# One chunked-attention and feed-forward kernel, its hand-written order of 801 steps replaced: v of the second unit behind the first weight cast on ScalarE, and all sequences, banks and engines drawn anew from there

## The chip, the cores and the metric

The kernel runs on one core of one Trainium2 chip. The metric is device time in microseconds, the median of several runs. A core has TensorE (PE, the matrix engine), VectorE (DVE), ScalarE (ACT), GpSimd (POOL) and SyncE (SP), which here only issues transfers; ACT issues transfers too. Each engine works through its own instructions in order, and waits on semaphores for the others.

## The reference

Inputs are q, k, v and alpha of 4 batches, 8 heads, 768 positions and 48 numbers a head, and four weight matrices. First a gated recurrence with a state of 48 x 48 for each head, then a feed-forward part whose hidden layer is the largest of three products:

```
for t in range(S):
    state = alpha[:, :, t, :, None] * state + einsum('bhd,bhe->bhde', k[:, :, t], v[:, :, t])
    y[:, :, t] = einsum('bhd,bhde->bhe', q[:, :, t], state)
x = y.transpose(0, 2, 1, 3).reshape(B * S, H * D)          # 3072 x 384
h = maximum(maximum(x @ w1, x @ w2), x @ w3)                # 3072 x 768
out = h @ w_out                                             # 3072 x 384
```

## The kernel before

The 768 positions are cut into 6 chunks of 128, and a **unit** is one chunk of one batch with its 8 heads: 24 units, numbered chunk by chunk, so units 0 to 3 are the first chunk of the four batches. Two units make a group, for which alpha, q, k and v are loaded: "load v 0 8" is v of the second half of group 0, which is v of unit 1. The first four groups are loaded in halves of 192 KB, the others in one piece of 384 KB.

For a unit u the steps are: "ln" (ACT, L402) takes logarithms of alpha; "cums u" (PE, L442) sums them along the chunk; "ep u" and "en u" (ACT, L447 and L450) are exponentials of these sums; "q~ u" and "k~ u" (L454, POOL or DVE) multiply q and k with them; "turn u" (PE, L483) transposes both and "qkT u" (L490, DVE or ACT) copies them out; "scores u" (PE, L499) multiplies them; "LA u" (DVE, L504) masks the scores; "v u" (L461 on ACT, L464 on POOL) scales v; "outs u" (PE, L542 and L545) makes the unit's output; "xb u" scales it (ACT L556, DVE L558); "x turn u" (PE, L572) and "xT u" (L577) transpose it for the second part. "totals", "e", "G", "sums", "U" and "Z" carry the state from chunk to chunk. In some late units a DMA transpose on SP ("cross u", "cross x u") stands in for PE's.

The second part takes the largest of three products as a sum: with differences wd = w2 - w1 and w3 - w1, the result is x w1 + max(0, x wd1, x wd2), so "grow u q g" (PE, L642) makes a product with one difference g of piece q, "relu" (ACT, L653) takes the first from 0 up and "max" (DVE, L658) takes the second in. The x w1 part is folded into one matrix w1 x w_out ("w1 turn", L366; "w1T", L372; "fold", L383; "w1o", L390). "shrink u" (PE, L678) makes the output rows, "ob u" (L693) copies them from PSUM and "store u" (L698) sends them off. Units 0 to 3, 22 and 23 go through this part alone, the rest in pairs.

The weights come in two column pieces, 0 to 256 (384 KB) and 256 to 768 (768 KB): "weights g p" is piece p of matrix g, where 0, 1, 2 are w1, w2, w3 and 3 is w_out. They arrive as fp32. "cast 0 p" and "cast 3 p" (ACT, L333) turn w1 and w_out into fp16, and "sub g p" (DVE or POOL, L341) makes the difference from the fp32 piece and the cast of w1. "grow" of a piece waits for its sub, the folds for all of the casts of w_out and the three w1T.

At the start PE also runs 27 "zeros" (L586): products of zeros, whose result nothing reads.

The order is written out by hand. The program enumerates 801 steps; ORDER is the list in which they are issued, and so fixes the sequence on each engine; PICK says for which steps the second of the offered engines is taken; BANKS gives each PSUM tile one of 8 banks (scores take two), in the order in which the tiles are enumerated. A tile that takes a bank waits until the readers of its former tile are done. The transfers of SP and ACT begin in the order of the list.

```
for i in ORDER:
    how, _, run, deps, _, _ = self.steps[i]
    e = how[PICK.get(i, 0)][0]
    ins = run(e)
```

Both kernels have the same steps, and so the same arithmetic and transfers.

Of the kernel before, what the change touches and what calls it, by code (L numbers as in the profile page):

```python
# [15 lines left out]

CDEC = 0.92
SIG = 128.0

NBANKS = 8  # L20
LEAD = (2.0, 4.0, 6.5, 5.0)
# [11 lines left out]


ORDER = (
# [44 lines left out]
)  # L80
BANKS = (
# [9 lines left out]
)  # L91
PICK = {
# [8 lines left out]
}  # L101


TRANSFERS = ("load", "weights", "cross", "store")
BEHIND = mybir.DependencyInfo(mybir.DependencyClass.NoSync, mybir.DependencyReason.DATA)
HARD, HARD_LOAD, HARD_LATE, LATE_FROM = 0.5, 1.8, 1.5, 3


# [18 lines left out]
class Plan:  # L127
# [31 lines left out]
    def issue(self, place):  # L159
        place.update(zip(self.users, BANKS))  # L160
        done, began = set(), []
        for i in ORDER:
# [4 lines left out]
            ins = run(e)  # L167
            if e != "POOL" and self.names[i].split()[0] in TRANSFERS:
                began.append(ins.ins)
# [5 lines left out]
def kernel(  # L175
# [41 lines left out]
    c32_np = np.stack(  # L217
        [SIG / dec, dec / SIG, np.full(P, HALF * np.log(CDEC))], axis=1
    ).astype(np.float32)
# [520 lines left out]
    for one, other in zip(began, began[1:]):  # L740
        tc.add_manual_dep(other, one.name, BEHIND, reason="transfers begin in the order of the plan")
# [28 lines left out]
```

## Time and profile before

| | before |
|---|---|
| median of 3 runs | 153.72 us (151.42 to 154.11) |
| profiled execution, device time | 150.59 us |
| its span in the profile | 148.8 us |
| PE busy | 133.9 us, 90% |
| DVE busy | 106.9 us, 72% |
| ACT busy | 90.5 us, 61% |
| POOL busy | 52.5 us, 35% |
| DMA | 31.07 MB, mean 209 GB/s |

A row of the timeline has the start, the duration, the engine (with a q where its queue issues a transfer), the line, the operation, what it writes and reads, the shape, the count, and in brackets how long the engine had been idle and what ended that. A row of the transfers ends with the us from issue to landing. A row of a stretch has, after its bounds and length, the busy us (and instructions) of PE, PE's weight loads, DVE, ACT and POOL, then the granted PE clock, the DMA engines' busy share and GB/s. A row of the groups has the instructions that share line, engine and shape, with their sum and the mean ns of one. Rows of the chain of waits have the start, the us, the engine and the line. The span runs from the first instruction to the last; the device time has some more around it.

### The profile page before, as it was taken

How to read it: one execution, taken by the hardware profiler on the slowest of the kernel's cores; microseconds unless marked ns; L12 is line 12 of the kernel's file. 1: busy time of each engine (PE TensorE's matmuls, PEld its weight loads, DVE VectorE, ACT ScalarE, POOL GpSimd, SP SyncE). 2: the span in 40 equal slices, each digit the busy share in tenths (PEclk: the TensorE clock that was granted, in tenths of full speed). 3: DMA queues.
4: the chain of work that ended last, by engine and by line, in shares of the span. 5: the costliest groups of instructions: out<-in, count | busy, mean ns of one | idle time of the engine just before them, and what ended most of it. 6: DMA issues, size and time to landing. Idle time of an engine off the chain costs nothing.

```text
span 148.8 us, 4162 instructions
## 1 busy us (share of the span) xinstructions
PE 133.9 (90%) x1683; PEld 104.6 (70%) x1683; DVE 106.9 (72%) x186; ACT 90.5 (61%) x184; POOL 52.5 (35%) x75
## 2 busy tenths in 40 slices
PE   0575297999999999999999999999999999999991
PEld 0233266968787886888787797787878877689781
DVE  7239318487998898979697779998578878584140
ACT  3531976948667587797746686745475844554331
POOL 0050041202523414840597709448029290170000
PEclk9999659999999999999999999999999999999999
DMA  5999999999999999999999999899998999704322
GB/s 115 205 225 322 202 341 269 283 267 173 223 208 219 237 220 210 248 184 250 266 266 263 185 197 250 163 215 269 177 232 160 243 325 189 147 4 131 109 82 79
DMA packets 116131, 31.07 MB, mean 209 GB/s; under 512 B 109712, under 2 KB 114960, under 8 KB 116112
## 3 DMA queue, kind: packets, MB, share of 16 engines
q1 hardware_dynamic: 83888, 21.17, 69.7%
q10 hardware_dynamic: 32224, 9.64, 28.7%
q8 instruction: 13, 0.21, 0.6%
q14 instruction: 6, 0.05, 0.1%
HBM read 23.69 MB, written 4.72 MB: 191 GB/s over the span
## 4 chain that ended last, share of the span: by engine, by line
PE 85%; SPq 5%; DMA 4%; ACT 2%; DVE 2%; issue 0%; ACTq 0%
PE psum L642 33%; PE psum L678 24%; PE psum L499 5%; PE psum L483 4%; SPq L308 4%; DMA vn<-in_v_dram 4%; PE psum L545 3%; PE psum L572 3%; PE psum L442 3%; PE psum L542 2%; PE psum L604 2%; PE psum L383 2%; PE psum L586 2%; PE psum L412 1%; DVE wd L341 1%; ACT w1h L333 1%
## 5 line engine op out<-in xcount | busy, mean ns | idle before, releaser
L642 PE MATMUL psum<-xT,wd 128*128 128x256 f16 (+1 forms) x540 | 54.4, 251 | 0.9 <-DVE wd L341 0.9
L642 PEld LDWEIGHTS <-wd 128*128 128x128 f16 x540 | 42.9, 98 | 6.9 <-DVE wd L341 1.7
L658 DVE TENSOR_TENSOR hT<-psum,hT 128x512 f16<-128x512 f32 (+1 forms) x39 | 24.3, 644 | 10.3 <-PE psum L642 4.7
L504 DVE TENSOR_TENSOR LA<-psum,c 128x1024 f16<-128x1024 f32 x24 | 28.6, 1219 | 3.1 <-PE psum L499 2.5
L653 ACT ACTIVATE hT<-psum 128x512 f16<-128x512 f32 (+1 forms) x39 | 21.5, 570 | 14.6 <-PE psum L642 13.6
L678 PE MATMUL psum<-wo,hT 128*128 128x384 f16 (+1 forms) x150 | 27.7, 320 | 0.0
L617 POOL TENSOR_TENSOR Z<-U,G 48x192 f16<-48x192 f32 x29 | 16.4, 572 | 12.5 <-DVE U L611 11.4
L678 PEld LDWEIGHTS <-hT 128*128 128x128 f16 x150 | 14.5, 98 | 8.9
L454 POOL TENSOR_TENSOR qk<-qn,ep 128x384 f16<-128x384 f32 x11 | 10.9, 998 | 15.1 <-ACT ep L447 13.3
L678 PE MATMUL psum<-w1o,xT 128*128 128x384 f16 (+1 forms) x75 | 15.8, 319 | 0.0
L450 ACT ACTIVATE en<-psum 128x384 f32<-128x384 f32 x24 | 11.9, 495 | 4.3 <-PE psum L442 3.8
L402 ACT ACTIVATE la<-an 128x384 f16<-128x384 f32 (+1 forms) x16 | 10.8, 689 | 5.7 <-DMA an<-in_alpha_dram 5.7
L454 POOL TENSOR_TENSOR qk<-kn,en 128x384 f16<-128x384 f32 x8 | 8.3, 1042 | 16.6 <-ACT en L450 12.7
L556 ACT ACTIVATE xb<-psum,c 128x384 f16<-128x384 f32 x16 | 9.1, 582 | 8.0 <-PE psum L545 5.8
L447 ACT ACTIVATE ep<-psum 128x384 f32<-128x384 f32 x24 | 11.7, 496 | 2.6 <-DVE qk L454 0.9
L693 ACT COPY ob<-psum 128x384 f32<-128x384 f32 (+1 forms) x18 | 8.3, 468 | 7.8 <-PE psum L678 5.1
L442 PE MATMUL psum<-la,c 128*128 128x384 f16 x24 | 7.8, 347 | 5.6 <-ACT la L402 5.5
L461 ACT ACTIVATE v<-vn,c 128x384 f16<-128x384 f32 x14 | 8.3, 614 | 6.2 <-DMA vn<-in_v_dram 6.2
L545 PE MATMUL psum<-v,LA 128*128 128x48 f16 x192 | 11.1, 186 | 0.0
L611 DVE TENSOR_TENSOR U<-psum,Z 128x384 f32<-128x384 f32 x16 | 8.5, 551 | 3.1 <-PE psum L604 2.5
L545 PEld LDWEIGHTS <-LA 128*128 128x128 f16 x192 | 9.8, 98 | 0.6 <-issue 0.2
L464 POOL TENSOR_SCALAR v<-vn,c 128x384 f16<-128x384 f32 x10 | 6.3, 635 | 9.4 <-DMA vn<-in_v_dram 9.0
(61 smaller groups left out, 189.6 us busy)
## 6 DMA issues: line engine op xcount, KB each, us to landing
out_dram<-ob ACTq DMA_DIRECT2D x20, 192.0 KB, 3.3
an<-in_alpha_dram SPq DMA_DIRECT2D x7, 384.0 KB, 6.6
ws<-in_moe_w_dram SPq DMA_DIRECT2D x3, 768.0 KB, 6.1
kn<-in_k_dram SPq DMA_DIRECT2D x5, 384.0 KB, 6.5
vn<-in_v_dram ACTq DMA_DIRECT2D x5, 384.0 KB, 6.6
an<-in_alpha_dram SPq DMA_DIRECT2D x8, 192.0 KB, 4.0
kn<-in_k_dram SPq DMA_DIRECT2D x8, 192.0 KB, 4.4
qn<-in_q_dram ACTq DMA_DIRECT2D x4, 384.0 KB, 5.3
```

The source lines that it names most:

```text
L402: lambda e, lo=lo * H, hi=hi * H: nc.scalar.activation(out=la[:, lo:hi, :D], in_=an[:, lo:hi, :], func=AFT.Ln, scale=1.0 / CDEC),
L442: nc.tensor.matmul(live[Lk], tri, la[:, hs, :D], start=True, stop=True)
L447: lambda e: nc.scalar.activation(out=ep, in_=live[Lk], func=AFT.Exp),
L450: lambda e: nc.scalar.activation(out=en, in_=live[Lk], func=AFT.Exp, scale=-1.0),
L454: lambda e, w=w, x=x, d=d: engines[e].tensor_mul(qk[:, w, :, :D], ld[x][n % LOADED][:, hs], d),
L504: lambda e: nc.vector.tensor_mul(LA.rearrange("p a b t -> p (a b) t"), live[Ak].rearrange("p a (b t) -> p (a b) t", t=P), maskA.unsqueeze( ...
L545: nc.tensor.matmul(yp[:, 2 * j + p, :], LA[:, p, j, :], v16[:, 2 * j + p, :], start=(cb == 0), stop=True, skip_group_check=True)
L617: lambda e, rows=rows, cols=cols: engines[e].tensor_mul(Zn[rows, :, cols], (Us[u % 3] if cb else live[pk])[rows, :, cols], G[rows, i * NP: ...
L642: nc.tensor.matmul(live[gk][:, jj, :], wd[:, kt, g, j * P:(j + 1) * P], xT[:, kt, :], start=(kt == 0), stop=(kt == NFT - 1))
L653: lambda e, h=h, gk=gk: nc.scalar.activation(out=h, in_=live[gk], func=AFT.Relu),
L658: lambda e, h=h, gk=gk: nc.vector.tensor_max(h, live[gk], h),
L678: nc.tensor.matmul(live[ok][:, cols], a[:, i * P:(i + 1) * P], w[:, cols], start=(kt == 0), stop=(kt == nk - 1))
```

## The change

ORDER, BANKS and PICK are replaced; two definitions move up in the file. The steps that are issued stay the same 801. 77 of them go to another engine, and 214 of 251 PSUM tiles to another bank. The heads of the lists:

```
 ORDER = (
-    4, 8, 9, 5, 6, 0, 10, 12, 34, 7, 32, 1, 11, 2, 123, 65, 127, 82, 84, 128, 129, 83, 64, 131,
-    86, 130, 85, 92, 115, 117, 98, 103, 104, 97, 95, 93, 68, 99, 133, 88, 110, 36, 37, 3, 42,
-    13, 87, 124, 70, 69, 35, 132, 33, 44, 73, 134, 89, 96, 106, 135, 90, 112, 56, 100, 136, 91,
...
+    5, 0, 8, 4, 12, 9, 2, 34, 6, 10, 11, 1, 37, 3, 32, 7, 65, 124, 64, 123, 82, 127, 83, 84,
+    129, 128, 86, 85, 131, 130, 92, 105, 104, 108, 99, 103, 97, 68, 88, 66, 116, 112, 94, 133,
+    106, 89, 132, 70, 69, 35, 72, 134, 71, 135, 90, 13, 36, 14, 136, 91, 42, 74, 93, 54, 107,
...
 BANKS = (
-    7, 1, 7, 7, 1, 4, 1, 3, 4, 3, 3, 4, 1, 2, 4, 6, 5, 0, 4, 3, 7, 0, 1, 5, 2, 5, 4, 6, 1, 5, 5,
...
+    3, 6, 3, 0, 1, 6, 0, 4, 2, 5, 4, 4, 0, 2, 3, 1, 2, 5, 2, 7, 7, 6, 7, 7, 7, 5, 4, 5, 5, 1, 4,
...
 PICK = {
-    27: 1, 30: 1, 44: 1, 71: 1, 72: 1, 75: 1, 85: 1, 86: 1, 87: 1, 132: 1, 138: 1, 140: 1, 144:
...
+    27: 1, 30: 1, 45: 1, 71: 1, 72: 1, 73: 1, 79: 1, 85: 1, 87: 1, 130: 1, 140: 1, 170: 1, 173:
...
```

Read as names, by following the enumeration, the fronts of the sequences are these (aN, kN, qN, vN: a load of unit N; Wgp: weights g p):

| | before | after |
|---|---|---|
| SP | a1 a2 k2 k1 q1 a0 q2 a3 W01 v1 W00 k0 v2 q0 W10 W11 v0 W31 k3 q3 W30 W21 W20 a4 | k1 a0 a2 a1 a3 k2 q0 W01 q1 q2 v2 k0 W11 v0 W00 v1 k3 W10 q3 W31 W30 W21 W20 a4 |
| ACT | ln 2, ln 1, en 1, ep 2, en 2, ep 1, ln 0, v 1, ln 3, en 0, ep 0, cast 0 1, v 2, cast 0 0, ep 3, qkT 0, xb 1, w1T 2, xT 2, w1T 1, w1T 0, e 1, xb 0, en 3, relu 2 1, cast 3 1, relu 1 1, e 0, relu 2 0, relu 1 0, cast 3 0 | ln 1, ln 3, ln 0, ln 2, ep 1, en 1, en 2, ep 2, en 0, ep 0, cast 0 1, w1T 1, xb 2, e 0, v 1, v 0, xb 1, en 3, cast 0 0, ep 3, w1T 2, relu 1 1, xT 2, e 1, w1T 0, cast 3 1, cast 3 0, relu 1 0, relu 2 1, relu 2 0, relu 0 0 |
| DVE | k~ 1, q~ 1, qkT 2, qkT 1, LA 2, LA 1, k~ 0, q~ 0, xb 2, LA 0, xT 1, sub 1 1, xT 0, q~ 3, qkT 3, LA 3, sub 2 1, sub 2 0 | q~ 1, q~ 2, qkT 1, k~ 0, qkT 2, q~ 0, LA 2, LA 1, qkT 0, LA 0, xT 1, sub 1 0, xb 0, xT 0, qkT 3, LA 3, sub 2 1, sub 2 0 |
| POOL | k~ 2, q~ 2, sub 1 0, v 0, k~ 3, v 3 | k~ 1, k~ 2, v 2, sub 1 1, k~ 3, q~ 3, v 3 |
| PE, zeros left out | cums 2, cums 1, cums 0, turn 2, turn 1, scores 2, scores 1, w1 turn 2, cums 3, turn 0, outs 1, outs 2, scores 0, w1 turn 1, x turn 2, x turn 1, w1 turn 0, outs 0, totals 1, grow 2 1 0, grow 2 0 0, x turn 0, grow 1 1 0, totals 0, grow 0 1 0, grow 1 0 0, turn 3, grow 0 0 0, scores 3, the folds, grow 0 1 1 | cums 1, cums 2, cums 0, turn 1, totals 0, turn 2, scores 2, scores 1, turn 0, w1 turn 1, outs 2, w1 turn 2, scores 0, outs 1, cums 3, x turn 1, outs 0, totals 1, grow 1 1 0, x turn 2, grow 1 0 0, x turn 0, turn 3, w1 turn 0, grow 0 0 0, scores 3, grow 2 0 0, grow 0 1 0, grow 2 1 0, the folds, grow 0 1 1 |

The 27 zeros stand between these steps in both; after, 13 of them stand between turn 1 and outs 1. Further on, PE's steps are permuted among near neighbours, by 13 places at most. Between DVE and POOL, ten q~ or k~ go to POOL (k~ 1, q~ 3, k~ 5, q~ 6, k~ 8, q~ 11, q~ 12, k~ 18, q~ 22, k~ 23) and eight to DVE (q~ 2, q~ 5, q~ 7, k~ 10, k~ 13, q~ 18, k~ 21, k~ 22); ten v go to POOL and three come from it; "sub 1 1" goes to POOL and "sub 1 0" to DVE. ACT has 12 steps fewer, four stores go from ACT to SP, and one load from SP to ACT.

More of the change, by code (lines that the diff above doesn't have):

```diff
@@ L18 @@
 SIG = 128.0
+TRANSFERS = ("load", "weights", "cross", "store")
+BEHIND = mybir.DependencyInfo(mybir.DependencyClass.NoSync, mybir.DependencyReason.DATA)
 NBANKS = 8
@@ L35 @@
 ORDER = (
[44 rows of a table removed]
[44 rows of a table added]
 )
 BANKS = (
[9 rows of a table removed]
[9 rows of a table added]
 )
 PICK = {
[8 rows of a table removed]
-}
-TRANSFERS = ("load", "weights", "cross", "store")
-BEHIND = mybir.DependencyInfo(mybir.DependencyClass.NoSync, mybir.DependencyReason.DATA)
[8 rows of a table added]
+}
 HARD, HARD_LOAD, HARD_LATE, LATE_FROM = 0.5, 1.8, 1.5, 3
```

112 rows, old and new, of tables (BANKS, ORDER, PICK) are left out of this document.

## The prediction

> **What bounds the kernel now.** I read the page first, then the busy time by stage, because the share of a whole span says little about a kernel with a filling stage and a long steady one. I cut the stages at the places where TensorE (PE) changes its manner: its first matmul, the end of its longest wait, and the matmul at 33.76 us that waits for the last weight difference. The two short windows at the end show the clock.
>
> ```profile
> span 148.8 us, 4162 instructions
> PEclk9999659999999999999999999999999999999999
> ...
> 5.54:17.71 12.17, 6.78 (x50) 3.28 (x49) 5.81 (x7) 5.72 (x12) 1.99 (x2) 0.93 1.05 241
> 17.71:33.76 16.05, 15.13 (x185) 11.20 (x186) 9.39 (x11) 12.04 (x23) 3.23 (x3) 0.84 1.03 288
> 33.76:145.78 112.02, 111.99 (x1449) 90.06 (x1449) 87.95 (x148) 70.90 (x149) 47.11 (x66) 1.00 1.01 200
> 145.78:148.80 3.02, 0.00 (x0) 0.00 (x0) 0.36 (x1) 0.00 (x0) 0.00 (x0) 1.00 0.29 98
> ...
> 16.00:18.00 2.00, 0.29 (x3) 0.30 (x4) 0.75 (x2) 2.00 (x3) 0.00 (x0) 0.50 0.87 190
> 22.00:24.00 2.00, 2.00 (x33) 1.67 (x30) 1.61 (x3) 0.80 (x3) 0.58 (x1) 0.81 1.10 349
> ```
>
> The first number after the stretch is its length, the next is PE's busy time, then PE weight loads, VectorE (DVE), ScalarE (ACT), GpSimd (POOL), then the granted clock, the DMA share and GB/s. From 33.76 to 145.78 us PE is busy for 111.99 of 112.02 us at full clock: after 33.76 there is no idle time for any order to take away. The last 3.02 us are the last copy and store. So the kernel is a fixed 112.02 us of PE work and a fixed end, put behind a filling stage; an order can only move the 33.76, or open gaps behind it. In the filling stage the DMA share is 1.05 and 1.03 of the 16 engines: that stage is bound by transfers. Now the chain that sets 33.76.
>
> ```profile
> 7.51 1.10 SPq L327 DMA_DIRECT2D ws<-in_moe_w_dram  x1
> 8.65 0.49 SPq L308 DMA_DIRECT2D vn<-in_v_dram  x1
> 9.81 0.91 SPq L308 DMA_DIRECT2D kn<-in_k_dram  x1
> 22.14 2.61 SPq L327 DMA_DIRECT2D ws<-in_moe_w_out_dram  x1
> 24.79 2.10 SPq L327 DMA_DIRECT2D ws<-in_moe_w_dram  x2
> ...
> ws<-in_moe_w_dram SPq DMA_DIRECT2D x1, 768.0 KB, 6.1
> vn<-in_v_dram SPq DMA_DIRECT2D x1, 192.0 KB, 5.8
> kn<-in_k_dram SPq DMA_DIRECT2D x1, 192.0 KB, 6.6
> ws<-in_moe_w_out_dram SPq DMA_DIRECT2D x1, 384.0 KB, 6.7
> ws<-in_moe_w_dram SPq DMA_DIRECT2D x1, 768.0 KB, 6.3
> ...
> 14.51 0.61 ACT L461 ACTIVATE v<-vn,c 128x384 f16<-128x384 f32 x1 [5.19 <-DMA vn<-in_v_dram]
> 15.03 0.51 ACT L402 ACTIVATE la<-an 128x384 f16<-128x384 f32 x1
> ...
> 15.81 0.48 ACT L447 ACTIVATE ep<-psum 128x384 f32<-128x384 f32 x1
> 16.18 1.47 ACT L333 CAST w1h<-ws 128x1536 f16<-128x1536 f32 x1
> 18.06 0.83 ACT L333 CAST w1h<-ws 128x768 f16<-128x768 f32 x1
> 29.43 0.86 ACT L333 CAST wo<-ws 128x768 f16<-128x768 f32 x1
> ...
> 17.71 0.82 PE L366 MATMUL psum<-c,w1h 128*128 128x128 f16 x6 [4.27 <-ACT w1h L333]
> 25.69 1.18 PE L642 MATMUL psum<-xT,wd 128*128 128x128 f16 x18 [0.90 <-DVE wd L341]
> 30.64 3.10 PE L383 MATMUL psum<-wo,w1T 128*128 128x384 f16 x18
> 33.76 1.18 PE L642 MATMUL psum<-xT,wd 128*128 128x128 f16 x18
> ...
> 30.81 1.23 DVE L504 TENSOR_TENSOR LA<-psum,c 128x1024 f16<-128x1024 f32 x1 [0.57 <-PE psum L499]
> 31.95 2.62 DVE L341 TENSOR_TENSOR wd<-ws,w1h 128x1536 f16<-128x1536 f32 x2
> L341 DVE TENSOR_TENSOR wd<-ws,w1h 128x1536 f16<-128x1536 f32 x2 | 3.5, 1749 | 0.0
> ```
>
> The DMA rows were read one issue at a time; the last number is us from issue to landing. So weights 0 1 (issued 7.51) land at 13.61, v of unit 1 at 14.45, k of unit 0 at 16.41, weights 3 0 at 28.84, weights 2 1 at 31.09. In the kernel before, "v 1" stands ahead of "cast 0 1" on ACT and waits 5.19 us for v; the cast, whose weights lay there since 13.61, starts at 16.18, and PE waits 4.27 us for it. That is the visible stall. But the end of the stage hangs on something else: the fold (30.64) needs "cast 3 0" of weights that land at 28.84, and the matmul at 33.76 needs "sub 2 1", of weights that land at 31.09. DVE began it at 31.95, behind LA 3, and one takes 1.749 us.
>
> **The change part by part.** 77 steps change engine and 214 of 251 tiles change bank, by counting the diff; the step set is the same. On PE the first 56 steps hold the same steps before and after in another order, then the folds (positions 56 to 58), then "grow 0 1 1". On SP the first 21 transfers are the same set, then weights 2 1. So bytes ahead of weights 2 1 are unchanged, and I leave its landing at 31.09, and weights 3 0 at 28.84.
>
> The prices of the moved kinds, POOL against DVE:
>
> ```profile
> L341 POOL TENSOR_TENSOR wd<-ws,w1h 128x768 f16<-128x768 f32 x1 | 1.6, 1639 | 9.3 <-DMA ws<-in_moe_w_dram 9.3
> L454 POOL TENSOR_TENSOR qk<-qn,ep 128x384 f16<-128x384 f32 x11 | 10.9, 998 | 15.1 <-ACT ep L447 13.3
> L454 DVE TENSOR_TENSOR ws<-qn,ep 128x384 f16<-128x384 f32 x4 | 2.3, 586 | 0.0
> L464 POOL TENSOR_SCALAR v<-vn,c 128x384 f16<-128x384 f32 x10 | 6.3, 635 | 9.4 <-DMA vn<-in_v_dram 9.0
> ```
>
> *The transfers.* Between k of unit 0 and weights 3 0 come 5 loads of 192 KB, 768, 384, 768 and 384 KB: 3264 KB in 12.43 us, 263 KB/us. In the new order weights 0 1 have 7 loads ahead in place of 8, so 0.73 us less: 12.9. Then q of unit 1 at 13.6, k of unit 0 at 15.7, weights 1 1 at 18.6, v of unit 0 at 19.3, weights 0 0 at 20.8, v of unit 1 (from tenth to sixteenth) at 21.5, k of unit 3 at 22.2, weights 1 0 at 23.7, q of unit 3 at 24.4, weights 3 1 at 27.4, weights 3 0 at 28.8. These are estimates at that rate, in order of issue.
>
> *The cast.* With v 1 behind it, cast 0 1 runs 12.9 to 14.4 (the ten steps ahead of it on ACT, at the 0.51 of the ln row, are done in 5.1 us after the fourth load, ahead of 12.9), 3.3 us earlier than its end of 17.65. Taken alone it would empty the 4.27 us wait. What is late next: PE's first turn now waits for q of unit 1, 13.6 plus one multiplication of about 0.6 (the 586 ns row), 14.2; so PE waits there, not at the weight turn. The next wait is "v 1" itself: v lands at 21.5, v 1 ends at 22.1 (0.61). Queued behind it on ACT are v 0, xb 1, en 3, cast 0 0 and ep 3, and PE stands at "outs 1".
>
> *PE up to outs 1.* Three turns, 13 zeros, three scores, two weight turns, one outs and one totals: at half clock 3 x 0.85 + 13 x 0.32 + 3 x 0.54 + 2 x 0.64 + 0.33 + 0.3 = 10.3 us. I take the pieces from the chain of waits, those at full clock doubled or nearly so:
>
> ```profile
> 21.62 0.54 PE psum L499 x8
> 20.02 0.32 PE psum L545 x8
> 29.07 0.45 PE psum L483 x8
> 26.87 0.16 PE psum L586
> 27.70 0.18 PE psum L412 x8
> ```
>
> (Scores and outs, 0.54 and 0.32, stood at half clock already; a turn of eight has 0.45, a zero 0.16, a totals 0.18 at full clock, and a weight turn is six of a turn's eight.) The clock before stood at 0.50 when PE resumed at 17.71 and the window 22 to 24 has a mean of 0.81, so 38% of it, to about 22.8, was still half: 5.1 us after the resumption. From 14.2 that gives 19.3, with 5.1 us done, and the remaining 5.2 us take 2.6: outs 1 is reached at 21.9, just as v 1 ends at 22.1. If the clock never rises, it is 24.5.
>
> *From there to the fold.* ACT: v 0 22.6, xb 1 23.0, en 3 23.4, cast 0 0 24.2, ep 3 24.6. "sub 1 0", now on DVE, needs that cast: 25.2. "sub 1 1", now on POOL, has twice the columns of the 1639 ns row: 3.3 us from 18.6, so 21.9, before outs 1 and so hidden. q~ 3 on POOL: 25.7; turn 3 from 26.0; weight turn 0 26.9; its copy, ahead of the wo casts on ACT: 27.8. Then cast 3 1 (1.47) to 29.3, cast 3 0 (0.86) to 30.1, fold 3.10 to 33.2. PE's own work from outs 1 to the fold is 6.5 us, so it is there by 30.1 with 1.5 us of these waits. DVE can do sub 2 1 from 31.09 to 32.84. "grow 0 1 1" therefore comes at 33.2: **0.5 us earlier** than 33.76. Bounds: not before 32.84, a gain of 0.9; with the cold 24.5 the chain shifts by 2.4 us to 35.6, a loss of 1.9. I take the 0.5, since the transfers and not PE set every other step of it.
>
> *After 33.76.* Nothing can be gained: 0.03 us of idle time in 112.02. What can be lost: ten of the q~ and k~ multiplications go from DVE to POOL and eight come back, ten v go to POOL and three leave it; ACT loses twelve steps.
>
> A multiplication takes 998 ns on POOL and 586 on DVE, 0.41 more; ten uncovered are 4.1 us, all covered nothing. A v takes 0.635 on POOL and 0.61 on ACT: no change. The cover is POOL's room, 47.11 of 112.02 us busy, and DVE's, 87.95. The new banks add waits for earlier readers, bounded the same way: 0 to 4.1 for all of it together. I take **0.8**, two such multiplications, nearer to nothing because POOL is far from full. Four stores go to SP, each issued where SP has only late transposes left; nothing. The end (last shrink, its copy, the store on SP) stays as it is.
>
> **The sum:** -0.5 + 0.8 = +0.3 us. The profiled execution took 150.59 us, 1.78 more than its span, so 150.9 for a like one; its run lay 3.13 under the median of the three runs shown, 153.72 (151.42 to 154.11). I carry the difference over: **154.0**.
>
> **The rivals.**
>
> *PE stays at half clock until the fold.* Place: outs 1. For: the new order leaves PE waiting at turn 1 and again at outs 1, and before, a wait of 4.27 us stood ahead of 0.50. Against: PE is full between 14.2 and 21.9. If it is cold to 24.5 and for 5.1 us more (2.55 of the 6.5 us done), the fold starts at 24.5 + 5.1 + 3.95 = 33.5, ends at 36.6 and the gate is 2.9 later; with the 0.8, +3.7: 157.4. It decides as soon as outs 1 comes after 24.5.
>
> The Trainium skill, "TensorE: Matmul & The Clock Gate", Part 1, says that half rate is the default, and that full rate comes after about 3.4 us of sustained work in a free-running window. By it outs 1 would be reached at 14.2 + 3.4 + 3.45 = 21.1, and v 1 at 22.1 would still decide; the trace has 5.1 in place of 3.4.
>
> *POOL and banks open gaps in the steady stage.* For: the stage is gapless, so each late producer counts in full. Against: POOL 42% busy. All ten uncovered: -0.5 + 4.1 = +3.6, 157.3. Beyond 3.6 us of idle time after the gate it decides.
>
> *Faster.* Most runs before took 3.13 us more than the profiled one. If that is one more stretch of half clock behind the 4.27 us wait, the earlier cast saves it in the median: 153.72 - 3.13 + 0.3 = 150.9. For: the spread of 2.7 us between runs of one program. Against: the new order waits too, at turn 1 and at outs 1.
>
> *The change does not do what it says:* the ACT wait for v is moved, not removed. That is inside the forecast.
>
> **How the numbers follow.** Forecast 0.58; half clock 0.17; gaps 0.12, of which 0.08 beyond 2%; faster 0.13. A measurement of this kernel can tell about 2%, 3.1 us, from no change. So faster 0.13, same 0.62, slower 0.17 + 0.08 = 0.25. The range reaches from the faster case, 150.9, to a little past both slow ones, 158.0; the forecast's own is 153.2 (gate -0.9 and a half-size gap) to 156.4 (+1.9 and 0.8).
>
> **What would show it.** Right: cast 0 1 ends near 14.4; ACT waits for v near 21.5; fold at 30 to 31; grow 0 1 1 at 33 to 34; less than 2 us of PE idle behind it. Wrong: sub 2 1's weights landing before 30; PEclk below 9 beyond slice 6; a gate past 35; or a steady stage shorter than 112 us.

## The result

After: 153.38 us, the median of 20 runs (151.93 to 155.03). Before, run beside it: 152.00 us (149.84 to 154.11, 20 runs). The ratio is **1.0126, interval 1.0102 to 1.0150** (it leaves disturbed executions out, and so is not the quotient of the two medians): slower by 1.3%, or 1.9 us, which is less than the 2% that the prediction took as the limit. The profiled execution took 152.77 us, 2.18 more than that of before.

The page of the kernel after, and its busy time by the same stretches (columns as before: length, busy us of PE, PE's weight loads, DVE, ACT and POOL, granted clock, DMA share, GB/s):

```profile
span 151.0 us, 4157 instructions
...
5.54:17.71 12.17, 6.88 (x44) 3.81 (x45) 3.25 (x6) 5.62 (x11) 2.54 (x3) 1.00 1.01 247
17.71:33.76 16.05, 14.04 (x196) 10.30 (x193) 10.71 (x13) 10.70 (x21) 5.51 (x3) 1.00 1.00 273
33.76:145.78 112.02, 110.66 (x1435) 88.70 (x1434) 87.90 (x150) 68.20 (x142) 49.48 (x71) 1.00 1.03 199
145.78:151.00 5.22, 2.14 (x18) 1.39 (x16) 0.92 (x2) 0.71 (x2) 0.00 (x0) 1.00 0.33 113
```

Behind 33.76, where PE was busy for all but 0.03 us before, it now is idle for 112.02 - 110.66 = 1.36 us, and 2.14 us of matmuls are left over at 145.78. In this execution the loss therefore stands behind the filling stage. The timeline of the filling stage after:

```profile
12.87 1.47 ACT L333 CAST w1h<-ws 128x1536 f16<-128x1536 f32 x1
22.01 1.12 ACT L461 ACTIVATE v<-vn,c 128x384 f16<-128x384 f32 x2 [0.75 <-DMA vn<-in_v_dram]
28.70 2.21 ACT L333 CAST wo<-ws 128x1536 f16<-128x1536 f32 x2
...
13.72 1.03 PE L483 MATMUL psum<-c,qk 128*128 128x128 f16 x8 [1.66 <-DVE qk L454]
19.99 0.81 PE L586 MATMUL psum<-Z 128*128 128x384 f16 x4
22.68 0.36 PE L545 MATMUL psum<-v,LA 128*128 128x48 f16 x8 [0.62 <-ACT v L461]
25.99 0.68 PE L642 MATMUL psum<-xT,wd 128*128 128x128 f16 x9 [0.46 <-DVE wd L341]
30.96 3.09 PE L383 MATMUL psum<-wo,w1T 128*128 128x384 f16 x18
33.88 1.17 PE L642 MATMUL psum<-xT,wd 128*128 128x128 f16 x18
```

The cast runs from 12.87, as the diff meant, and the 4.27 us wait at the weight turn is gone. PE waits 1.66 us at turn 1 for q~ 1 and 0.62 at outs 1 for v 1 in its place, and reaches the gate ("grow 0 1 1") at 33.88 in place of 33.76: 3.3 us on ACT came to nothing at the gate. The waits of PE behind the gate:

```profile
PE psum L545 <- ACT v L461: 0.5, 1, 0.5
PE psum L642 <- DMA xT<-xb: 0.4, 1, 0.4
PE psum L483 <- ACT ob L693: 0.3, 1, 0.3
```

And in the timeline:

```profile
58.97 0.61 PE L483 MATMUL psum<-c,ws 128*128 128x128 f16 x8 [0.35 <-ACT ob L693]
114.28 2.13 PE L642 MATMUL psum<-xT,wd 128*128 128x256 f16 x18 [0.38 <-DMA xT<-xb]
116.95 0.21 PE L545 MATMUL psum<-v,LA 128*128 128x48 f16 x2 [0.50 <-ACT v L461]
```

Two of them are ends of transfers: the DMA transpose of x 16, and "v 19" on ACT, which waited for its load. The third, turn 9, the profile puts down to a copy on ACT; but turn 9 neither reads that copy nor takes the bank that it reads (its bank was last read by "ep 9" and "en 9"). It reads q~ 9, and this ends last, on DVE (rows of DVE, POOL and ACT):

```profile
57.51 1.37 DVE L454 TENSOR_TENSOR ws<-qn,ep 128x384 f16<-128x384 f32 x1
...
57.45 1.00 POOL L454 TENSOR_TENSOR ws<-qn,ep 128x384 f16<-128x384 f32 x1
...
116.29 0.61 ACT L461 ACTIVATE v<-vn,c 128x384 f16<-128x384 f32 x1 [2.70 <-DMA vn<-in_v_dram]
```

q~ 9 ends at 58.88 and the turn begins at 58.97. It takes 1.37 us, with POOL multiplying beside it; in the timeline of the kernel before the same one takes 0.55 (rows of DVE and PE, the second is turn 9):

```profile
58.75 0.55 DVE L454 TENSOR_TENSOR ws<-qn,ep 128x384 f16<-128x384 f32 x1
...
60.07 0.61 PE L483 MATMUL psum<-c,ws 128*128 128x128 f16 x8
```

The longer multiplication alone does not make the wait. Before, q~ 9 ended later, at 59.30, and PE came to turn 9 later still, at 60.07: there "shrink 4", nine matmuls, and "x turn 6" stand ahead of turn 9, and the new order has them behind it.

"v 19" stands behind the 2.70 us that ACT waits for a load in the last row of after.

### The profile page after: what moved, and what is told of

It is laid out like the page before. It is cut to its first block, busy times and chain, and to the rows that moved or that the text cites. A ratio compares the mean times of both kernels' runs of the same rounds, so it can differ in the third digit from the quotient of the medians.

```text
span 151.0 us, 4157 instructions
## 1 busy us (share of the span) xinstructions
PE 133.7 (89%) x1683; PEld 104.3 (69%) x1683; DVE 106.1 (70%) x189; ACT 86.5 (57%) x175; POOL 57.7 (38%) x81
## 4 chain that ended last, share of the span: by engine, by line
PE 74%; DMA 10%; SPq 9%; ACT 2%; DVE 1%; issue 1%; DVEq 0%
PE psum L642 30%; PE psum L678 22%; DMA vn<-in_v_dram 10%; SPq L308 7%; PE psum L483 4%; PE psum L499 4%; PE psum L545 3%; PE psum L542 2%; PE psum L442 2%; PE psum L572 2%; PE psum L383 2%; PE psum L604 2%; SPq L327 2%; PE psum L412 1%; ACT v L461 1%
## 5 line engine op out<-in xcount | busy, mean ns | idle before, releaser
L464 POOL TENSOR_SCALAR v<-vn,c 128x384 f16<-128x384 f32 x17 | 10.0, 593 | 23.0 <-DMA vn<-in_v_dram 20.6
L617 POOL TENSOR_TENSOR Z<-U,G 48x192 f16<-48x192 f32 x26 | 13.5, 526 | 11.7 <-DVE U L611 11.0
L454 POOL TENSOR_TENSOR qk<-kn,en 128x384 f16<-128x384 f32 x10 | 10.2, 1032 | 14.1 <-ACT en L450 13.2
L693 ACT COPY ob<-psum 128x384 f32<-128x384 f32 (+1 forms) x16 | 7.4, 470 | 10.0 <-PE psum L678 5.1
L454 DVE TENSOR_TENSOR qk<-qn,ep 128x384 f16<-128x384 f32 x7 | 4.1, 592 | 9.0 <-DMA qn<-in_q_dram 8.9
L556 ACT ACTIVATE xb<-psum,c 128x384 f16<-128x384 f32 x13 | 7.6, 583 | 4.8 <-PE psum L545 4.5
L483 PE MATMUL psum<-c,qk 128*128 128x128 f16 x96 | 8.2, 235 | 1.7 <-DVE qk L454 1.7
```

Of the source, the lines that this page charges most:

```text
L454: lambda e, w=w, x=x, d=d: engines[e].tensor_mul(qk[:, w, :, :D], ld[x][n % LOADED][:, hs], d),
L483: nc.tensor.transpose(live[tk][:, w, j, :], qk[:, w, 2 * j:2 * j + 2, :], ident)
L617: lambda e, rows=rows, cols=cols: engines[e].tensor_mul(Zn[rows, :, cols], (Us[u % 3] if cb else live[pk])[rows, :, cols], G[rows, i * NP: ...
```

## The experiments

Each ratio is to the kernel before, run beside it on the same chip. Where only orders are joined, a few banks were chosen anew, as otherwise two tiles would meet in one.

**The stated edit alone.** v 1 (87) behind cast 0 1 (35), in the order of before; nothing else.

```
-    13, 87, 124, 70, 69, 35, 132, 33, 44, 73, ...
+    13, 124, 70, 69, 35, 87, 132, 33, 44, 73, ...
```

> The kernel before with one move: v 1 behind cast 0 1 on ScalarE, nothing else. Theory A (transfers set the gate, the matmul that waits for sub 2 1): cast 0 1 starts at about 13.6 in place of 16.2, TensorE's wait of 4.27 us falls below 2.5, but the gate stays between 33.0 and 33.8, so the ratio to before is 0.995 to 1.000. Rival B (the wait of 4.27 us is a real loss): all of the 2.6 us that the cast gains reach the end, ratio 0.983.

Measured: 150.90 us, **0.9960 (0.9928 to 0.9993)**, the only version of the case with the full work that is faster than before. PE's timeline:

```profile
14.27 0.51 PE L366 MATMUL psum<-c,w1h 128*128 128x128 f16 x6 [0.98 <-ACT w1h L333]
18.30 0.82 PE L483 MATMUL psum<-c,qk 128*128 128x128 f16 x6 [3.20 <-DVE qk L454]
25.63 1.18 PE L642 MATMUL psum<-xT,wd 128*128 128x128 f16 x18 [0.41 <-DVE wd L341]
33.69 0.68 PE L642 MATMUL psum<-xT,wd 128*128 128x128 f16 x9
```

The cast ends 3.4 us earlier and the weight turn with it; then PE waits 3.20 us at turn 0 for q of unit 0, and from 25.63 it runs unbroken to a gate at 33.69, 0.07 earlier. The stall moves to the next late load, as theory A has it, and not the 0.983 of rival B.

**The two halves of the new order.** Both orders have the same steps in their first 134 places, so they can be cut there.

```
-ORDER = BEFORE
+ORDER = AFTER[:134] + BEFORE[134:]     # new fill
+ORDER = BEFORE[:134] + AFTER[134:]     # new steady stage
```

> The changed order, engines and banks for the 134 steps ahead of the folds, those of before from there (three banks at the seam chosen anew). Theory A: the fill is neutral, gate 33.6 to 34.2, ratio 0.998 to 1.003. Rival C (the fill loses, as TensorE starts later and waits at turn 1 and outs 1, more in most runs than in the profiled one): ratio 1.010 or more.

> The order, engines and banks of before for the 134 steps ahead of the folds, the changed ones from there (five banks at the seam chosen anew). Theory A: the loss sits here, ratio 1.010 to 1.014, with late waits at turn 9, at the first grow of unit 16 and at outs 19. Rival C: ratio 1.000 to 1.003.

Measured: new fill 151.53 us, 1.0025 (0.9988 to 1.0062), gate at 34.03; new steady stage 152.80 us, 1.0074 (1.0030 to 1.0117). The new fill is worth nothing that can be told from nought, the new steady stage costs 1.1 us; with the fill's 0.4 that is 1.5 of the 1.9 us. The first is as theory A has it; the second lies between the two expectations. Whether its waits are the expected ones is not shown.

**The edit undone in the new order.** After, with v 1 ahead of cast 0 1 again.

```
-    ..., cast 0 1, w1T 1, xb 2, e 0, v 1, v 0, ...      (ACT, as names)
+    ..., v 1, cast 0 1, w1T 1, xb 2, e 0, v 0, ...
```

> The changed kernel with v 1 put back ahead of cast 0 1 on ScalarE, its load staying sixteenth. Theory D (the wait is only moved, and the move of the load is what makes the edit necessary): v 1 still ends near 22.6, the cast near 24.1, the first weight turn behind it, gate 36 to 38.5, ratio to before 1.03 to 1.05. Rival E (the fill has room, transfers alone set the gate): gate below 35, ratio below 1.02.

Measured: 158.24 us, 1.0458 (1.0407 to 1.0509). ACT and PE:

```profile
21.96 0.61 ACT L461 ACTIVATE v<-vn,c 128x384 f16<-128x384 f32 x1 [8.92 <-DMA vn<-in_v_dram]
22.48 1.46 ACT L333 CAST w1h<-ws 128x1536 f16<-128x1536 f32 x1
...
23.99 0.82 PE L366 MATMUL psum<-c,w1h 128*128 128x128 f16 x6 [3.30 <-ACT w1h L333]
39.16 1.00 PE L642 MATMUL psum<-xT,wd 128*128 128x128 f16 x15
```

In the new order, where v of unit 1 is the sixteenth transfer, the place of "v 1" is worth 5.3 us at the gate (39.16 against 33.88), which is past the 36 to 38.5 that theory D expected; the ratio is in its range. The new order needs the edit; the old one gains 0.6 us by it.

**POOL's longer multiplication.** After, with the seven q~ and k~ behind the gate that had gone to POOL and take 1.0 us there, back on DVE.

```
+q~ 6, k~ 8, q~ 11, q~ 12, k~ 18, q~ 22, k~ 23: VectorE
```

> The changed kernel with seven of the q~ and k~ that it moved to GpSimd (q~ 6, k~ 8, q~ 11, q~ 12, k~ 18, q~ 22, k~ 23) back on VectorE, order and banks as changed. Theory P (the longer multiplication on GpSimd, 1.0 against 0.59 us, is what the steady stage loses): ratio to before 1.004 to 1.007. Rival O (the loss is in where steps and transfers stand in their queues, as the waits at turn 9, grow 16 and outs 19 say): no gain, 1.011 to 1.017, VectorE getting fuller.

Measured: 154.71 us, 1.0187 (1.0142 to 1.0232). No gain, and more than even rival O expected: putting the seven back wins nothing, though what POOL's 0.41 us of extra length costs by itself is not separated from what a fuller DVE costs. This run also shows the half-clock rival, in a filling stage identical to that of after (PE's timeline; lines of this kernel stand one lower):

```profile
21.56 1.45 PE L587 MATMUL psum<-Z 128*128 128x384 f16 x4
24.45 0.36 PE L546 MATMUL psum<-v,LA 128*128 128x48 f16 x8
35.65 0.55 PE L643 MATMUL psum<-xT,wd 128*128 128x128 f16 x7
75.29 0.62 PE L484 MATMUL psum<-c,ws 128*128 128x128 f16 x8 [1.51 <-DVE ws L455]
```

Its stretch from 20 to 22 us:

```profile
20.00:22.00 2.00, 2.00 (x20) 1.48 (x18) 1.73 (x3) 0.87 (x2) 2.00 (x1) 1.00 0.95 187
```

The same four zeros take 1.45 us here and 0.81 at 19.99 in the kernel after. PE is at half pace to about 23.8, reaches outs 1 at 24.45, and the gate comes at 35.65. Behind it, turn 11 waits 1.51 us for DVE: the multiplications that were put back make DVE late.

**Two sites put back.** After, with turn 9, its copy and scores 9 where before had them, and load v 9 ahead of load k 10 on ACT.

```
+turn 9, qkT 9 behind x turn 6; scores 9 behind turn 8
+load v 9 0 ahead of load k 10 0
```

> The changed kernel with two sites mended: turn 9 and scores 9 stand on TensorE where before had them, and the load of v for units 18 and 19 stands ahead of the load of k for units 20 and 21 on ScalarE's queue. Theory O: the 0.35 us wait at turn 9 and the 0.7 us wait inside outs 19 go, and ratio to before falls from 1.0126 to about 1.005 to 1.008. Rival M (the transfer engines are full until 130 us, so a transfer that goes ahead only makes another one late): the wait at outs 19 goes but grow 16 or a later step waits instead, ratio 1.010 to 1.014.

Measured: 157.01 us, 1.0322 (1.0262 to 1.0383): a miss. The waits at turn 9 and outs 19 are gone, as expected, but behind the load that was moved ahead the next issue on ACT takes long:

```profile
99.91 0.45 ACTq L308 DMA_DIRECT2D vn<-in_v_dram  x1
100.40 3.20 ACTq L308 DMA_DIRECT2D kn<-in_k_dram  x1
103.64 0.87 ACT L450 ACTIVATE en<-psum 128x384 f32<-128x384 f32 x2 [3.53 <-DMA out_dram<-ob]
...
104.18 0.48 PE L604 MATMUL psum<-v,qk 128*128 128x96 f16 x4 [2.72 <-ACT en L450]
```

The issue of k takes 3.20 us, to 103.60, and "en" stands behind it on ACT and begins at 103.64. It is what PE waits 2.72 us for. The profile names a store, finished at last, as what let it go.

**Twelve zeros earlier.** The first experiment's order, with 12 of the zeros moved behind "cums 3", to fill its 3.20 us wait and keep the clock up.

```
+zeros 9 19 24 22 21 16 15 10 2 13 17 26 behind cums 3
```

> The kernel before with v 1 behind cast 0 1, and twelve zeros, which stood behind turn 0, moved ahead of it behind cums 3, into the 3.2 us in which TensorE waited there. Theory F (with the cast early, TensorE is busy without a break from 25.6 to the gate at 33.7, so four zeros behind 25.6 cost 0.16 us each, and the zeros keep the clock up): clock 1.00 up to 20 us, gate 33.0 to 33.2, ratio 0.989 to 0.993. Rival A (transfers alone set the gate): gate 33.6 or later, ratio 0.996 to 0.998.

Measured: 152.27 us, 1.0023 (0.9986 to 1.0060): a miss. Timeline of POOL and PE:

```profile
23.56 2.17 POOL L464 TENSOR_SCALAR v<-vn,c 128x384 f16<-128x384 f32 x1 [1.40 <-DMA vn<-in_v_dram]
...
25.78 0.36 PE L545 MATMUL psum<-v,LA 128*128 128x48 f16 x8 [2.51 <-POOL v L464]
```

PE came to outs 0 earlier and waited 2.51 us there: v of unit 0 had landed at 23.47, and "v 0" took 2.17 us on POOL, which takes 0.635 in the mean of before's ten, while DVE made a weight difference. So about 1.5 of the 2.51 us are POOL's longer time, and the rest is the late load.

**New from two thirds on.** Before up to its 566th step, after from there.

```
+ORDER = BEFORE[:566] + the steps left, as AFTER has them
```

> Order, engines and banks of before for the first 566 steps (to about 100 us), the changed ones from there. Reading of the one profile (1.1 of the 2.2 us lost behind 100 us, at grow 16 and outs 19): ratio 1.006 to 1.008. Rival (the late transfers behind these waits were made late earlier, between 40 and 100 us, so the last third alone costs nothing): 0.999 to 1.003.

Measured: 157.54 us, 1.0340 (1.0274 to 1.0406): inconclusive, since the cut makes a loss of its own. One store and one load stand on other sides of the cut in the two orders, and the timeline shows an output copy that waits for the former store of its buffer:

```profile
106.70 0.48 ACT L693 COPY ob<-psum 128x384 f32<-128x384 f32 x1 [5.88 <-DMA out_dram<-ob]
...
107.23 1.03 PE L642 MATMUL psum<-xT,wd 128*128 128x256 f16 x8 [3.09 <-ACT ob L693]
```

**Fewer bytes.** Both orders, with the loads of q and v cut from group 4 on.

```
+                end = lo + 1 if x in "qv" and n >= LOADED else hi
-                              t[:, lo:hi],
+                              t[:, lo:end],
```

> The kernel before, with each load of q and of v from group 4 on cut to the first of its 16 heads (its output is not the reference's for these groups); all 801 steps, their order, banks, engines and waits stay. This takes 2 x 8 x 360 KB = 5.9 MB of 31.07 MB away. It is the partner of the next run. The kernel before has 0.03 us of idle time behind the gate, so both theories expect little: 0.995 to 1.000 of its time, DMA share falling from 1.0 to about 0.75 between 40 and 115 us.

> The kernel after, with the same loads cut in the same way (its output is not the reference's for these groups). Theory T (the +2.0 us in the steady stage comes mostly from loads, stores and transposes that land later because the transfer engines are full): the waits at grow 16 0 0 (0.38) and at outs 19 (0.5) go, only turn 9's 0.35 for q~ 9 on VectorE stays, and the time stands at 1.002 to 1.005 of the run before it, idle behind the gate 0.3 to 0.7 us. Rival O (the loss is in the order of arithmetic, banks and engines, and the late transfers are only beside it): it stays at 1.010 to 1.014 of the run before it, with about 2 us of idle time behind the gate.

Measured: 150.68 us, 0.9954 (0.9925 to 0.9983), and 152.55 us, 1.0068 (1.0036 to 1.0099); the second to the first is 1.0068/0.9954 = 1.011, by the two intervals 1.007 to 1.016 (an estimate). With 19% fewer bytes nearly the whole loss stays, and at least half of it. Stretches of the order after with fewer bytes:

```profile
60.00:90.00 30.00, 29.82 (x390) 23.76 (x388) 26.40 (x43) 19.20 (x40) 20.85 (x32) 1.00 0.54 123
90.00:120.00 30.00, 30.00 (x378) 23.98 (x376) 25.01 (x43) 18.88 (x40) 11.24 (x14) 1.00 0.75 160
```

And all of PE's waits behind the gate, one line, turn 9 (lines of this kernel stand one lower):

```profile
PE psum L484 <- ACT ob L694: 0.3, 1, 0.3
```

As the theory of late transfers expected, the DMA share falls to 0.54 and 0.75, and the waits at grow 16 and outs 19 are gone; but the time does not follow. These waits are not the greater part of what the median loses. Nor are there the rival's 2 us of idle time behind the gate: of the 1.83 us between the two profiled executions at the start of PE's last group of matmuls (146.51 and 144.68), 1.15 stand at the gate already (34.17 and 33.02).

**The queues of before.** After, with the five transfers that had changed queue put back.

```
+store 14 0, 16 0, 19 0, 23 0: ScalarE;  load q 9 0: SyncE
```

> The kernel after, with the five transfers that changed queue put back to the queue of before: stores 14, 16, 19 and 23 issued by ScalarE, load q 9 by SyncE; nothing else changed. Theory Q (the queue that issues a transfer makes it late, since an issue that finds its queue full holds up what stands behind it): the waits at outs 19 and at grow 16 shrink and the steady stage loses 1.0 us or less, ratio 1.004 to 1.008. Rival T (it is the bytes and their order): no difference from the kernel after, 1.011 to 1.015. Rival M (a store on ScalarE's queue blocks its arithmetic): above 1.016.

Measured: 153.37 us, 1.0108 (1.0071 to 1.0146). The stretches:

```profile
33.76:60.00 26.24, 25.84 (x362) 20.64 (x361) 20.54 (x36) 18.73 (x40) 10.03 (x15) 1.00 1.12 214
60.00:90.00 30.00, 29.81 (x391) 23.81 (x392) 26.87 (x44) 19.26 (x41) 20.26 (x30) 1.00 1.05 212
90.00:120.00 30.00, 30.00 (x377) 23.79 (x375) 25.19 (x44) 18.57 (x39) 11.74 (x16) 1.00 1.16 218
```

With all the bytes there, and the full DMA share of 1.05 and 1.16, the two late waits are gone as well: PE is idle 0.59 us up to 90 (26.24 - 25.84 and 30.00 - 29.81) and not at all behind. The ratio is 0.2% below after's 1.0126, above the range of theory Q and just short of rival T's. So the two waits come and go with small shifts in the transfers, and what stays in this execution is idle time ahead of 90 us and a gate at 34.64, 0.88 us later than before's.

**Turn 9 later.** The same, and turn 9, qkT 9 and scores 9 at before's places.

```
+turn 9, qkT 9 behind x turn 6; scores 9 behind turn 8
```

> The run before it (the kernel after with the five transfers on their old queues), and in it also turn 9 with its copy qkT 9 moved behind x turn 6, and scores 9 behind turn 8, as the kernel before has them; nothing else. Theory D (behind the gate, the loss that every execution shows is PE reaching turn 9 before VectorE has done q~ 9, 0.33 us, and what it puts on turns 10 and 11, 0.4 us): the wait at turn 9 goes, the idle time behind the gate falls from 1.1 us to 0.3 to 0.5, and the ratio to 1.005 to 1.008. Rival N (VectorE is late by itself, so the wait moves to the next step that needs it, turn 10 or scores 9): idle stays at 0.9 to 1.2 and the ratio at 1.009 to 1.013.

Measured: 152.84 us, 1.0086 (1.0050 to 1.0122): neither theory is excluded. Stretches:

```profile
33.76:60.00 26.24, 26.17 (x365) 20.92 (x363) 20.63 (x36) 18.86 (x40) 10.04 (x15) 1.00 1.08 208
60.00:90.00 30.00, 29.75 (x392) 23.76 (x390) 27.15 (x44) 19.56 (x41) 20.07 (x30) 1.00 1.06 216
```

One row of PE's timeline:

```profile
119.14 0.34 PE L572 MATMUL psum<-c,xb 128*128 128x128 f16 x3 [0.51 <-ACT xb L556]
```

Turn 9's wait goes (0.07 us idle to 60, where it was 0.40), the small ones around turns 10 and 11 stay (0.25), and a wait of 0.51 us, not there before, opens at x turn 19.

## Why the prediction was right or wrong

Its answer, no change beyond 2%, was right and 153.38 lies close to 154.0, but part of that is chance. The prediction stood on the 153.72 us of three runs; beside the kernel after, before took 152.00. The forecast **change** was +0.3 us and the measured one +1.9 (1.4 between the medians): the base was 1.7 us too high, and the sum of the change 1.1 to 1.6 us too low, and the two errors nearly cancel.

*What bounds the kernel:* right behind the gate, wrong ahead of it. PE's 112 us behind the gate were gapless, and an order could only move the gate or open gaps; in the profiles of the edit alone and of the run "new fill" the gate moved by 0.3 us at most. But the prediction hung the gate on the landings of weights 3 0 and 2 1, and took it that "the transfers and not PE" set the steps up to it. In its own profile PE is busy from 25.69 to 33.76 for 8.04 of 8.07 us and waits for neither, though the weight difference of 2 1 ends only 0.06 us ahead of the gate (31.95 + 1.749). In the new fill the gate goes with outs 1: in six of seven profiled executions it lies 11.20 or 11.21 us behind it, with outs 1 anywhere from 22.68 (after) to 24.45 (seven on DVE). In five of the seven PE comes to outs 1 too late to wait there for v 1. So the step that does not hold is the one from the landings to the gate; in its place the runs show the moment at which outs 1 begins, which in most of them is when PE gets there, behind a stretch at half pace.

*Transfers and cast:* near, in part by luck. The forecast had the cast at 12.9 to 14.4, turn 1 at 14.2, v 1 ending at 22.1, outs 1 at 21.9 to 22.1; the rows have 12.87 to 14.34, 13.72, 22.6 and 22.68. It had weights 2 1 unchanged at 31.09; they landed at 31.78. It had the cast begin as its weights land, at 12.9; they landed at 12.1 (issued at 6.64, 5.5 us), and the cast waited until ACT was done with "ep 0".

*From outs 1 to the fold:* mis-sized. Outs 1 comes 0.6 us late. PE's own work behind it was put at 6.5 us; it is 30.96 - 22.68 less waits of 0.51 (x turn 1) and 0.46 (grow 1 0 0), 7.3 us, while these waits were put at 1.5. The w_out casts end at 30.91, not 30.1. The fold comes 0.9 us and the gate 0.7 us later than worked out, and the gate term is +0.12 in place of -0.5.

*Half clock until the fold*, at 0.17: it does happen, as a spread between executions of one fill. In seven profiled executions of the new fill the gate lies at 33.88, 34.03, 34.17, 34.42, 34.64, 35.18 and 35.65; the last has PE at half pace nearly all the way to outs 1, at 24.45 against 24.5, and is the bound that the prediction gave for that, 35.6 or 1.9 us later than 33.76. The rival's 2.9 supposed half pace for 5.1 us more behind outs 1, which none of the seven has: in the last, the scores at 23.94 already take 0.40 us, as those at 21.39 in after. Two of the seven gates lie past 35, which the prediction named as a sign that it is wrong, and one within its 33 to 34. Of the old fill three executions have 33.02, 33.76 and 34.23. The Trainium skill, "TensorE: Matmul & The Clock Gate", Part 1, says that the window that decides is free-running, so that the change of pace falls differently in each run. The executions agree that it does, with half pace to 16.6 in after and to about 23.8 in the run with seven multiplications on DVE, but these lie 7 us apart where the section has half a microsecond either way.

*After 33.76:* this term, 0.8, was too small in after's execution. From the gate to the start of PE's last group of matmuls it is 111.35 us before (145.11 - 33.76) and 113.38 after (147.26 - 33.88): +2.03. By the same rows it is +0.68 with fewer bytes (against the old order with fewer bytes), +1.11 with the old queues, +1.48 with turn 9 later; but in these three the gate itself comes later, by 1.15, 0.88 and 0.66 us. So the two stages share the loss differently from one execution to the next. By the halves, in the median, the fill misses its -0.5 by 0.9 us and the steady stage its 0.8 by 0.3.

Of after's 2.03 us, 1.33 are idle time (1.36 less 0.03): 0.88 at grow 16 and outs 19, where transfers land late, 0.35 at turn 9, where PE comes too early for q~ 9, and small rests. The other 0.7 us are no idle time: behind 33.76 PE is busy for 110.66 + 2.14 us, of which 0.12 lie ahead of the gate, against 111.99 before, for the same matmuls. The prediction held this work to be fixed; no run shows why it grew, and as the profile models the ends of matmuls, its size is rough.

The mechanism that the prediction priced, POOL's longer multiplication, is in none of the waits of after: q~ 9 ran on DVE, and with the seven put back on DVE nothing is gained. It had DVE 87.95 of 112.02 us busy and took that as room; what it did not price is that DVE's own multiplication takes 1.37 us in place of 0.55 when POOL multiplies at the same time. Its 586 ns is the mean of four multiplications; others of before's 21 on DVE take up to 1.35 us.

*The change does not do what it says:* as forecast, ACT's wait for v moved, and is 0.75 us in place of 5.19; on PE it is outs 1.

*Four stores to SP, nothing:* in the median it held, 1.0108 with the queues put back against 1.0126, intervals overlapping.

*Faster*, at 0.13, by a half-clock stretch saved in the median: it fell. The 3.13 us stood on three runs; against 20 runs of before, the profiled execution lay 1.41 us under the median. With the visible stall removed alone, the time falls by 0.4%, not by 1.8%.

**Left open:** how the 1.9 us divide. The halves give 0.4 and 1.1, with half-widths of 0.6 and 0.7 us. The wait at turn 9 is shown in the profile, but its removal moved the median by only 0.2%, within the interval. Neither the later gate nor PE's longer busy time was taken away by any run, and so what causes the 1.1% that stays with fewer bytes is not shown. That half pace at outs 1 sets the gate is read from seven executions; no run held the pace fixed.

## What to carry to other kernels

A long visible stall in a filling stage is not the gain: the edit that removed 3.3 of 4.27 us brought 0.6, since PE ran into the next late load; look for the last point at which the engine starts to run unbroken, and ask what releases that. Where the engine that sets the end has no idle time, a fresh order of the whole program can only lose there, so keep the old order and edit it: one step moved beat 801 rearranged. And before a median is predicted from another run's span, ask how well the base itself is known; here it moved by as much as the change.

## What the runs showed of the hardware

- **DVE and POOL hold each other up.** q~ 9 on DVE began at 57.51, 0.06 us behind a multiplication on POOL, and ended at 58.88, 0.43 behind its end. "v 0" on POOL, in the run with earlier zeros, began 0.04 behind a weight difference on DVE and took 2.17 us:

```profile
23.52 1.75 DVE L341 TENSOR_TENSOR wd<-ws,w1h 128x1536 f16<-128x1536 f32 x1
```

It ended at 25.73, 0.46 behind the difference. In both the second takes the rest of the first and most of its own time. The profile of the kernel before has it too (rows of DVE and POOL): a multiplication on DVE that begins beside one on POOL takes 1.07 us and ends 0.41 behind it.

```profile
8.14 1.07 DVE L454 TENSOR_TENSOR qk<-qn,ep 128x384 f16<-128x384 f32 x1 [0.56 <-ACT ep L447]
...
7.80 1.00 POOL L454 TENSOR_TENSOR qk<-kn,en 128x384 f16<-128x384 f32 x1 [7.36 <-ACT en L450]
```

The Trainium skill, "SBUF — State Buffer", "SBUF: two separate sides", says that a DVE operation with two inputs in SBUF and a GpSimd operation that reads SBUF exclude each other for a whole instruction, the one that starts first going ahead. All three cases agree. The prediction weighed POOL's length against DVE's (0.41 us), and not this.
- **A transfer's issue can hold up arithmetic.** In the run with two sites put back, the issue of the load put ahead took 0.45 us on ACT and the issue behind it 3.20 us; ACT was idle for 3.53 us, and its next computation began 0.04 us behind the end of that issue.
- **The granted clock reads 1.00 while PE is still at half pace at the start.** In the run with seven on DVE the zeros take double at 21.56 with 1.00 in the stretch 20 to 22; with the old queues they take double with 0.50 in the record. Its row of PE:

```profile
20.59 1.46 PE L586 MATMUL psum<-Z 128*128 128x384 f16 x4
```

The stretch:

```profile
20.00:22.00 2.00, 2.00 (x17) 1.13 (x15) 1.00 (x2) 1.84 (x5) 1.62 (x1) 0.50 1.14 209
```

In the run with seven on DVE the first rise is seen only in the length of the matmuls; with the old queues the column shows the later fall.
